# Scores in pairs, unbroken blocks on TensorE, and all weights' low halves by one VectorE operation, in a block-sparse attention with an FFN behind it

## The chip, the cores and the metric

The kernel runs on one core of one Trainium2 chip. The metric is the device time of one execution in microseconds (us). Three runs of the kernel before gave 951.11, 952.15 and 955.74 us; their median is 952.15. One further execution was profiled.

A core has five engines that run side by side and wait for each other by semaphores: PE (TensorE, matrix multiplication, whose loads of the stationary operand are listed as PEld), DVE (VectorE), ACT (ScalarE), POOL (GpSimd) and SP (SyncE, which here issues the DMA transfers). Each takes its instructions in a fixed order.

## The reference

```python
B, H, S, D = 4, 8, 768, 64          # batch, heads, sequence, head dimension
block = 32; n_blocks = 24; 3 sampled key blocks for each query block
scores = q @ k.transpose / sqrt(D)
mask  = neighbouring blocks (|i - j| <= 1), first and last block as query or key, sampled blocks
attn  = softmax(where(mask, scores, -1e9))
x     = (attn @ v) with the heads side by side          # 3072 tokens x 512
h     = x @ w_in                                        # 512 -> 2048
out   = maximum(0.01 * h, h) @ w_out                    # 2048 -> 512
```

All inputs and the output are float32 (the sampled blocks are integers).

## The kernel before

Every float32 operand of a matrix product is split into a high and a low half in float16, after a scaling by a power of two; a product is then three (FFN) or four (attention) matmuls in float16, added up in PSUM. A score is two matmuls for each head, with both halves stacked along the 128 rows.

**Attention.** The queries are cut into tiles of 64 (two blocks), 12 tiles (T = 0 to 11) for each batch, and the heads into four pairs hp. One *unit* is one tile and one pair of heads: 4 x 12 x 4 = 192 units. Tile 0 holds the first and the last block, which see all 768 keys: its units have two *parts* of 384 keys. All other units have one part, whose 384 keys (12 blocks of 32) are gathered into kg and vg beforehand. So there are 208 parts. Two neighbouring units (u.pi 0 and 1) are a *pair*; four tiles are an *item* of 256 tokens (12 items).

The way of a unit:

- `unit_scores` (L613 to L633): four matmuls a part into one of two PSUM buffers of the pool ps_s, each with 64 output columns of the array (128*64 in the profile), one for each head of the pair, once for qs and once for qxs.
- `unit_ttr` (L639, DVE): mask and scaling, the row's extreme mx; with it the PSUM buffer is free again. `unit_exp` (L650, ACT): the exponential and its sum. `pair_norm` (L658, L659, DVE): the reciprocals for both units of a pair.
- `unit_high` (L665, ACT) and `unit_split` (L670, DVE): the high and the low half of the probabilities, pp; then a transposing DMA from SP's queue (L673) into pt.
- `pair_av` (L691, PE): 24 matmuls for a pair (12 a unit), again 64 columns wide. `tile_evac` (L700 to L711) makes x from it.

**FFN.** It goes in chunks of two 128-wide slices of the hidden dimension, 8 chunks for each item: `ffn_h` (24 matmuls, L726), `ffn_act1`, `ffn_max`, `ffn_act2` (ACT L733, DVE L737 and L742, POOL L743) and `ffn_o` (12 matmuls, L753). Both use the full 128*128 array. 96 chunks are 2304 and 1152 matmuls.

**Weights.** w_in and w_out are loaded in eight parts (four quarters of each), decoded in place by ACT and DVE (L292 to L298), their scale found by matmuls of each block with itself (L172) and L175, and then split in `finish` (L340). ACT writes the high half (L353). For the low half there are two ways, chosen by a letter of `CFG["wsplit"]` for each part: "p" scales the raw values in place on ACT (L355) and subtracts on POOL (L356); "d" does both in one SCALAR_TENSOR_TENSOR on DVE (L358). Parts 0 to 5 come in two groups of 1024 columns each, parts 6 and 7 in four of 512; the last part always takes a third way (L348 to L351).

**Order of the work.** The main loop makes one step for each unit. In each step it emits pieces in the order of `CFG["ord"]`, "dtsixScmgovabphw": among them t (unit_ttr), s (split), S (the scores of the next unit), o (ffn_o), a (the attention-times-V of a pair at least three steps old), h (ffn_h) and w (some of the weights' work). Every emitted instruction has a priority that grows with the emission (`tc.cur_priority`). A planner then fixes each engine's order: it walks through the instructions by a model of their durations, and gives each engine the ready one of the smallest priority. So what is emitted as one block, 24 matmuls of h for instance, may be broken by other instructions that become ready in between.

The functions that the diff touches, and what calls them:

Of the kernel before, what the change touches and what calls it, by code (L numbers as in the profile page):

```python
# [13 lines left out]
F32 = mybir.dt.float32  # L14
# [5 lines left out]
P = 128  # L20
# [8 lines left out]
KEYS = SLOTS * BLOCK  # L29
# [20 lines left out]
    "rmin": 0.0,  # L50
    "side": 1.2,
    "side0": 1.6,
    "spread": 8,
    "v_at": 28,
    "wr": [(0, 1.0), (4, 3.0), (10, 4.0), (18, 4.5)],
    "wsplit": "ppppppdd",
    "xbufs": 3,
}

# [2 lines left out]
def tile_block_sparse_attention_ffn(  # L62
# [87 lines left out]
    def scales(ss, n, name, **how):  # L150
        now = tc.cur_priority
        tc.cur_priority = now - CFG["bs"]
        begin = len(nc.cur_bb.bb.instructions)
        pb = scale_sum(ss, n, name)
        loose.update(i.name for i in nc.cur_bb.bb.instructions[begin:])
        r = scale_of(pb, n, name, **how)
        tc.cur_priority = now + 8
        return r

    eye = cst.tile([P, P], BF16, name="eye")  # L160

# [448 lines left out]
    class Unit:  # L610
        pass

    def unit_scores(u):  # L613
        i, c0 = u.k // 2, u.k % 2 * Q2
        require_qk(u.b, u.j, i, u.hp)
        if u.T:
            require_kg(u.b, u.T)
        key = (u.b, u.j, i, u.hp)
        if key not in nscale:
            score_scale(*key)  # L620
        u.nsc = nscale[key]
        qs, qxs, _ = qstack[u.b, u.j, i]
        u.sp = []
        for part in range(u.parts):
            sp = ps_s.tile([P, 512], F32, tag="s", name=f"s_{u.nm}_{part}")[:, :KEYS]
            for n, st in enumerate((qs, qxs)):
                for hh in range(2):
                    h = 2 * u.hp + hh
                    keys = kgs[u.b, u.T][0][:, h, :] if u.T else kts[u.b][:, h, part * KEYS:(part + 1) * KEYS]
                    nc.tensor.matmul(  # L630
                        sp[hh * D:(hh + 1) * D, :], st[:, h, c0:c0 + Q2], keys,
                        start=(n == 0), stop=(n == 1))
            u.sp.append(sp)  # L633

    def unit_ttr(u):
        u.p = [pa.tile([P, KEYS], F32, tag="p", name=f"p_{u.nm}_{i}", bufs=CFG["p"]) for i in range(u.parts)]
# [42 lines left out]
    def pair_av(pr):  # L679

        if pr.hp == 0:
            avs[pr.item.n, pr.T] = bank(f"av_{pr.nm}", "av").rearrange("p (n l t) -> p n l t", n=NP, l=2)
        pr.av = avs[pr.item.n, pr.T]
        for u in pr.units:
            require_v(u.b, u.hp, u.T)
            n = NCH * u.parts
            for c in range(n):
                for l in range(2):
                    for hh in range(2):
                        vt = vgs[u.b, u.T][:, c, 2 * u.hp + hh, :] if u.T else v16s[u.b, u.hp][:, c, hh, :]  # L690
                        nc.tensor.matmul(  # L691
                            pr.av[hh * D:(hh + 1) * D, u.hp], vt[:, l * D:(l + 1) * D],
                            u.pt[c // NCH][:, :, c % NCH, hh * D:(hh + 1) * D],
                            start=(c == 0 and l == 0), stop=(c == n - 1 and l == 1))

    def tile_evac(pr):

# [20 lines left out]
    def ffn_h(c):  # L718
        it = c.item
        c.ph = bank(f"h_{it.nm}_{c.f}").rearrange("p (f t) -> p f t", f=2)  # L720
        for i in range(2):
            f = c.f + i
            b, o = f // PER, (f % PER) * P
            for d in range(NP):
                for m, (wl, xl) in enumerate(((1, 0), (1, 1), (0, 0))):
                    nc.tensor.matmul(  # L726
                        c.ph[:, i], W16[:, 2 * b, d, wl, o:o + P], it.x[:, xl, d, :],
                        start=(d == 0 and m == 0), stop=(d == NP - 1 and m == 2))

    def ffn_act1(c):  # L730
        scale = down[c.f // PER] if c.whole else (GDOWN, 0.01 * GDOWN)
# [12 lines left out]

    def ffn_o(c):
        it = c.item
        for t in range(N2 // P):
            if c.first:
                it.po[t] = ps_o.tile([P, DM], F32, tag="o", name=f"o_{it.nm}_{c.f}_{t}")
            for i in range(2):  # L750
                f = c.f + i
                for m, (gl, wl) in enumerate(((0, 1), (0, 0), (1, 1))):
                    nc.tensor.matmul(  # L753
                        it.po[t], c.g[:, gl, i, t * P:(t + 1) * P], W16[:, 2 * (f // PER) + 1, f % PER, wl, :],
                        start=(c.first and i == 0 and m == 0), stop=(c.last and i == 1 and m == 2))
            if c.last:
                outs.append((it, t, it.po[t], c.qs))

    betas = {}

# [53 lines left out]
    def require_qk(b, j, i, hp):  # L814
        until(("k", b, hp), lambda: (b, hp) in kready)
        until(("q", b, j, i), lambda: (b, j, i) in qstack)

    def require_kg(b, T):
        for hp in range(NP):
            until(("k", b, hp), lambda: (b, hp) in kready)  # L820
        until(("kg", b, T), lambda: (b, T) in kgs)
# [177 lines left out]
    for u in units:  # L999
        it, ui = u.item, u.k * NP + u.hp  # L1000
        b, nb = it.b, it.b + 1

        if step == 2:
            start_q(1)
        if step == 6 or step % 8 == 3 and step > 8:
            get_q((step + 5) // 8 + 1)
        if step % 8 == 6:
            start_q(step // 8 + 2)
        if nb < B:
            g = it.j * 16 + ui  # L1010
            t = g - (CFG["k_at"] if b else CFG["k_at0"])
            if t % 5 == 0 and 0 <= t // 5 < NP:
                get_k(nb, t // 5)
            if t % 5 == 3 and 0 <= t // 5 < NP:
                start_k(nb, t // 5)
            t = g - CFG["v_at"]
            if t in (0, 2, 4, 6):
                load_v(nb, t // 2)
            if t == 8:
                start(("v", nb), prep_v(nb))  # L1020

        if u.hp == (CFG["g_at"] if step >= 4 else NP - 1) and u.T + 1 < NT:
            start_gather(b, u.T + 1)
        tc.cur_priority = max(tc.cur_priority, 1000 + step * 200)
        if step in ready:
            add_ffn(ready.pop(step))
        refill()
        backlog = len(hq) + sum(len(t[1]) for t in tasks)
        credit += max(CFG["rmin"], min(CFG["rmax"], backlog / CFG["spread"]))
        n = int(credit)  # L1030
        credit -= n
        if step == 0:
            unit_scores(u)
        c = aq[0] if aq else None
        for w in CFG["ord"]:
            if w == "c" and c:
                ffn_act1(c)
            elif w == "m" and c:
                ffn_max(c)
            elif w == "g" and c:  # L1040
                ffn_act2(c)
                oq.append(aq.popleft())
            elif w == "S" and step + 1 < len(units):
                unit_scores(units[step + 1])
            elif w == "t":
                while live[0] + u.parts > CFG["p"]:
                    if not pend_high and not pend_split:
                        norm_step()
                    high_step()
                    split_step()  # L1050
                live[0] += u.parts
                unit_ttr(u)
            elif w == "x":
                unit_exp(u)
                if u.pi == 1:
                    pend_norm.append(u.pair)
            elif w == "d":
                norm_step()
            elif w == "i":
                high_step()  # L1060
            elif w == "s":
                split_step()
            elif w == "a":
                av_step()
                if vq and vfree[0] and (vq[0][0], "ready") in scr:
                    start_gather_v()
            elif w == "v":
                ev_step()
            elif w == "b":
                do_out()  # L1070
            elif w == "o":
                do_o(CFG["flag"] if hq or aq else 0)
            elif w == "p":
                side_step(CFG["side0"] if step < 16 else CFG["side"])
                gather_step(2)
            elif w == "w":
                wcredit += [r for a, r in CFG["wr"] if step >= a][-1]
                while wcredit >= 1.0:
                    c = next(weights, "end")
                    wcredit -= c if c != "end" else wcredit  # L1080
            elif w == "h":
                for i in range(n):
                    if i:
                        do_act()
                        do_o(CFG["flag"])
                    do_h()
        step += 1
        if ui == 15:
            ready[step + CFG["lead"] if it.n else step + CFG["lead0"]] = it
# [62 lines left out]
```

## Time and profile before

| | |
|---|---|
| median of three runs | 952.15 us |
| the profiled execution's own time | 950.05 us |
| its span, first to last instruction | 948.4 us |
| mean granted TensorE clock | 0.928 |
| PE busy | 780.1 us, 82% |
| DVE busy | 625.1 us, 66% |
| ACT busy | 492.7 us, 52% |
| POOL busy | 329.0 us, 35% |
| last decoding of weights (L298) ends | 204.9 us |
| last L639 of attention ends | 873.8 us |

A row of the groups reads: source line, engine, operation, out<-in by the program's names, shapes, xcount, then busy time in all and mean ns of one, then the engine's idle time just before them and what ended it. A row of the timeline reads: start and length in us, engine, line, operation, names, shape, xcount of the merged instructions, and in brackets the idle time before it with what released it. Ends of matmuls are modelled and overlap the next one's start, so starts are what to compare. A row of the waits reads: who waited, for whom, us in total, times, longest. In the slices, one digit is the busy share of a fortieth of the span (23.7 us) in tenths, and PEclk is the granted clock in tenths of full speed.

### The profile page before, as it was taken

Reading aid. Unit: us, or ns where it says so; the run is one execution under the profiler, and the core shown is the slowest. Engines: PE = TensorE matmul, PEld = TensorE weight load, DVE = VectorE, ACT = ScalarE, POOL = GpSimd, SP = SyncE. Lnnn points to the kernel's source line nnn. Section 1 sums busy time; section 2 is a strip of 40 time slices with the busy share of each in tenths; the row PEclk is TensorE's granted clock in tenths of the full one; section 3 lists DMA queues with packets and bytes.
Section 4 is the critical chain, followed back from the end, with each engine's and each line's share of the span. In section 5 each row is a group of like instructions: output and inputs, shape, how many; then the busy total and the mean of one; then the engine's idle time right before and its main releaser. Section 6 shows DMA issues by size and latency. Waiting matters only on the chain. (4 is left out here: it accounts for less than half of the span.)

```text
span 948.4 us, 21924 instructions
## 1 busy us (share of the span) xinstructions
PE 780.1 (82%) x7020; PEld 491.3 (52%) x7020; DVE 625.1 (66%) x1691; ACT 492.7 (52%) x1061; POOL 329.0 (35%) x469
## 2 busy tenths in 40 slices
PE   1335536889979988989989878997998989999998
PEld 0213324445646545655556545654555555656674
DVE  4889699998767866556666666566566766655221
ACT  4566656675545545546544645555445654545121
POOL 0134554542213434343414242442314342432221
PEclk9996657789998989999999989999999999999999
DMA  9995698777877766776884978866784765655200
GB/s 212 289 277 142 160 254 183 152 155 140 162 176 139 149 140 140 157 125 138 148 167 110 175 132 141 162 133 137 151 163 112 149 137 127 119 122 124 34 23 23
DMA packets 358129, 139.39 MB, mean 147 GB/s; under 512 B 323965, under 2 KB 336254, under 8 KB 358014
## 3 DMA queue, kind: packets, MB, share of 16 engines
q1 hardware_dynamic: 358014, 137.99, 69.7%
q8 instruction: 55, 0.90, 0.4%
q14 instruction: 60, 0.49, 0.2%
HBM read 65.57 MB, written 12.58 MB: 82 GB/s over the span
## 5 line engine op out<-in xcount | busy, mean ns | idle before, releaser
L726 PE MATMUL h<-x,W 128*128 128x256 f16 x2304 | 294.2, 284 | 0.4 <-DVE ht L737 0.4
L753 PE MATMUL o<-W,g 128*128 128x512 f16 x1152 | 281.1, 386 | 3.6 <-DVE ob L773 1.4
L726 PEld LDWEIGHTS <-W 128*128 128x128 f16 x2304 | 228.6, 103 | 55.0 <-issue 8.0
L670 DVE SCALAR_TENSOR_TENSOR pp<-p,r,pp 128x384 f16<-128x384 f32 x208 | 153.0, 746 | 131.4 <-ACT pp L665 130.5
L743 POOL TENSOR_TENSOR g<-ht,g 128x512 f16<-128x512 f32 x96 | 116.3, 1212 | 289.1 <-DVE g L742 199.4
L665 ACT ACTIVATE pp<-p,r 128x384 f16<-128x384 f32 x208 | 121.5, 608 | 142.3 <-DMA pt<-pp 105.7
L575 POOL COPY kg<-kt 128x256 f16 x264 | 127.6, 505 | 145.2 <-PE s L630 91.0
L753 PEld LDWEIGHTS <-g 128*128 128x128 f16 x1152 | 105.1, 99 | 134.9 <-issue 25.3
L650 ACT ACTIVATE p<-p,mx 128x384 f32<-128x384 f32 x208 | 126.5, 608 | 88.6 <-DVE mx L639 56.3
L691 PE MATMUL av<-pt,vg 128*64 128x128 f16 x2112 | 97.6, 233 | 33.1 <-DMA pt<-pp 26.5
L639 DVE CUSTOM_DVE_ANT_0 p<-s,em,nsc 128x384 f32<-128x384 f32 x176 | 106.3, 609 | 23.3 <-PE s L630 22.0
L691 PEld LDWEIGHTS <-vg 128*64 128x64 f16 x2112 | 78.6, 117 | 70.4 <-issue 58.5
L630 PE MATMUL s<-kg,qs_q 128*64 128x384 f16 x352 | 66.5, 367 | 26.8 <-DVE mx L639 25.1
L737 DVE SCALAR_TENSOR_TENSOR ht<-h,gd,ht 128x512 f32<-128x512 f32 x80 | 59.6, 745 | 41.5 <-ACT ht L733 41.1
L733 ACT ACTIVATE ht<-h,gs 128x512 f32<-128x512 f32 x80 | 54.2, 677 | 60.9 <-PE h L726 50.2
L711 POOL TENSOR_TENSOR x<-xf,x 128x256 f16<-128x256 f32 x48 | 35.7, 744 | 128.7 <-ACT x L709 128.4
L630 PEld LDWEIGHTS <-qs_q 128*64 128x64 f16 x416 | 28.8, 115 | 93.0 <-issue 63.1
L630 PE MATMUL s<-kg,qxs_q 128*64 128x384 f16 x352 | 65.0, 352 | 0.0
L742 DVE CAST g<-ht 128x512 f16<-128x512 f32 x96 | 41.5, 432 | 8.8 <-PE o L753 7.8
L506 ACT ACTIVATE qn_q<-rq 128x512 f16<-128x512 f32 x24 | 15.1, 628 | 55.4 <-DMA rq<-in_q_dram 55.2
L650 ACT ACTIVATION_READ_ACCUMULATOR p<-p,mx 128x1 f32 x208 | 39.0, 187 | 0.0
L658 DVE TENSOR_SCALAR sum<-sum 128x2 f32<-128x2 f32 x96 | 24.9, 259 | 19.0 <-ACT p L650 18.4
(128 smaller groups left out, 744.4 us busy)
## 6 DMA issues: line engine op xcount, KB each, us to landing
vg<-scr SPq DMA_DIRECT2D x280, 64.0 KB, 1.9
vg<-scr SPq DMA_DIRECT2D x44, 256.0 KB, 3.0
v<-in_v_dram SPq DMA_DIRECT2D x32, 192.0 KB, 3.4
scr<-v SPq DMA_DIRECT2D x16, 384.0 KB, 3.6
W<-in_moe_w_in_dram SPq DMA_DIRECT2D x5, 1024.0 KB, 6.7
rq<-in_q_dram SPq DMA_DIRECT2D x20, 256.0 KB, 3.7
out_dram<-ob SPq DMA_DIRECT2D x20, 256.0 KB, 2.4
rk<-in_k_dram SPq DMA_DIRECT2D x24, 192.0 KB, 3.4
```

What stands on the lines that cost most here:

```text
L575: nc.gpsimd.tensor_copy(out=kg[:, :, slot * BLOCK:(slot + 1) * BLOCK], in_=kt[:, :, bass.ds(off, BLOCK)])
L630: nc.tensor.matmul(sp[hh * D:(hh + 1) * D, :], st[:, h, c0:c0 + Q2], keys, start=(n == 0), stop=(n == 1))
L639: nc.vector.tensor_tensor_reduce(out=u.p[i], in0=u.sp[i], in1=kgs[u.b, u.T][1] if u.T else zero.to_broadcast([P, KEYS]), scale=u.nsc, scal ...
L650: nc.scalar.activation(u.p[i], u.p[i], AF.Exp, scale=-1.0, bias=u.mx[:, :1], accum_out=u.pair.sum[:, u.pi, i:i + 1])
L665: nc.scalar.activation(pp[:, 0, :], p, AF.Copy, scale=u.r)
L670: nc.vector.scalar_tensor_tensor(out=pp[:, 1, :], in0=p, scalar=u.r, in1=pp[:, 0, :], op0=ALU.mult, op1=ALU.subtract)
L691: nc.tensor.matmul(pr.av[hh * D:(hh + 1) * D, u.hp], vt[:, l * D:(l + 1) * D], u.pt[c // NCH][:, :, c % NCH, hh * D:(hh + 1) * D], start=( ...
L726: nc.tensor.matmul(c.ph[:, i], W16[:, 2 * b, d, wl, o:o + P], it.x[:, xl, d, :], start=(d == 0 and m == 0), stop=(d == NP - 1 and m == 2))
L733: nc.scalar.activation(c.t, c.ph, AF.Copy, scale=scale[1])
L737: nc.vector.scalar_tensor_tensor(out=c.t, in0=c.ph, scalar=scale[0], in1=c.t, op0=ALU.mult, op1=ALU.max)
L743: nc.gpsimd.tensor_tensor(out=c.g[:, 1], in0=c.t, in1=c.g[:, 0], op=ALU.subtract)
L753: nc.tensor.matmul(it.po[t], c.g[:, gl, i, t * P:(t + 1) * P], W16[:, 2 * (f // PER) + 1, f % PER, wl, :], start=(c.first and i == 0 and m ...
```

## The change

Three things are changed.

1. `unit_scores` becomes `scores(us)`, which takes a list of units. At a step with u.pi == 1 the scores of the next two units, which are the next pair, are emitted together, the second unit's matmuls first; at a step with u.pi == 0 nothing is emitted, since that unit's partner was done with it. Units of tile 0 (two parts each) still come one by one.
2. A new function `together` takes a list of emitters. All instructions after the first get a priority far ahead of everything else, and an order edge that places them behind the first. So the planner starts a block when its first instruction is its turn, and then places the others before anything else that is ready. It is used for the scores, for `pair_av` (where the second unit's matmuls now come first), for `ffn_h` and for `ffn_o`.
3. `wsplit` is "dddddddd": parts 0 to 5 take the way with one DVE operation too.

```diff
+    "spair": 1,
-    "wsplit": "ppppppdd",
+    "wsplit": "dddddddd",
...
+    def together(emits):
+        now = tc.cur_priority
+        begin = len(nc.cur_bb.bb.instructions)
+        for n, emit in enumerate(emits):
+            if n == 1:
+                tc.cur_priority = now - 100000
+            emit()
+        new = nc.cur_bb.bb.instructions[begin:]
+        for i in new[1:]:
+            tc.add_manual_dep(i, new[0].name, mybir.DependencyInfo(
+                mybir.DependencyClass.NoSync, mybir.DependencyReason.DATA), reason="together")
+        tc.cur_priority = now + len(new)
...
-    def unit_scores(u):
+    def scores(us):
+        emits = []
+        for u in us:
...
+            u.sp = [ps_s.tile([P, 512], F32, tag="s", name=f"s_{u.nm}_{part}")[:, :KEYS] for part in range(u.parts)]
+        for u in us[::-1]:
...
+                        emits.append(lambda o=sp[hh * D:(hh + 1) * D, :], a=st[:, h, c0:c0 + Q2], k=keys, n=n:
+                                     nc.tensor.matmul(o, a, k, start=(n == 0), stop=(n == 1)))
+        together(emits)
...
     def pair_av(pr):
...
+        for u in pr.units[::-1]:
...                       # the 24 matmuls as emitters, in the order c, l, hh as before
+        together(emits)
...
     def ffn_h(c):         # and ffn_o(c): the same matmuls in the same order as emitters
...
+        together(emits)
...
             elif w == "S" and step + 1 < len(units):
-                unit_scores(units[step + 1])
+                ahead = units[step + 1:step + 3]
+                if not CFG["spair"]:
+                    scores(ahead[:1])
+                elif u.pi == 1:
+                    if any(x.parts > 1 for x in ahead):
+                        for x in ahead[:1]:
+                            scores([x])
+                    else:
+                        scores(ahead)
+                elif u.parts > 1:
+                    scores(ahead[:1])
```

More of the change, by code (lines that the diff above doesn't have):

```diff
@@ L611, in tile_block_sparse_attention_ffn @@
         pass
-    def unit_scores(u):
[L614 to L633, printed above, removed]
+    def scores(us):
+        emits = []
+        for u in us:
+            i, c0 = u.k // 2, u.k % 2 * Q2
+            require_qk(u.b, u.j, i, u.hp)
+            if u.T:
+                require_kg(u.b, u.T)
+            key = (u.b, u.j, i, u.hp)
+            if key not in nscale:
+                score_scale(*key)
+            u.nsc = nscale[key]
+            u.sp = [ps_s.tile([P, 512], F32, tag="s", name=f"s_{u.nm}_{part}")[:, :KEYS] for part in range(u.parts)]
+        for u in us[::-1]:
+            i, c0 = u.k // 2, u.k % 2 * Q2
+            qs, qxs, _ = qstack[u.b, u.j, i]
+            for part, sp in enumerate(u.sp):
+                for n, st in enumerate((qs, qxs)):
+                    for hh in range(2):
+                        h = 2 * u.hp + hh
+                        keys = kgs[u.b, u.T][0][:, h, :] if u.T else kts[u.b][:, h, part * KEYS:(part + 1) * KEYS]
+                        emits.append(lambda o=sp[hh * D:(hh + 1) * D, :], a=st[:, h, c0:c0 + Q2], k=keys, n=n:
+                                     nc.tensor.matmul(o, a, k, start=(n == 0), stop=(n == 1)))
+        together(emits)
     def unit_ttr(u):
@@ L685, in pair_av @@
             require_v(u.b, u.hp, u.T)
+        emits = []
+        for u in pr.units[::-1]:
             n = NCH * u.parts
@@ L690, in pair_av @@
                         vt = vgs[u.b, u.T][:, c, 2 * u.hp + hh, :] if u.T else v16s[u.b, u.hp][:, c, hh, :]
[L691 to L694, printed above, removed]
+                        emits.append(lambda o=pr.av[hh * D:(hh + 1) * D, u.hp], a=vt[:, l * D:(l + 1) * D],
+                                     m=u.pt[c // NCH][:, :, c % NCH, hh * D:(hh + 1) * D], c=c, l=l, n=n:
+                                     nc.tensor.matmul(o, a, m, start=(c == 0 and l == 0), stop=(c == n - 1 and l == 1)))
+        together(emits)
     def tile_evac(pr):
@@ L720, in ffn_h @@
         c.ph = bank(f"h_{it.nm}_{c.f}").rearrange("p (f t) -> p f t", f=2)
+        emits = []
         for i in range(2):
@@ L725, in ffn_h @@
                 for m, (wl, xl) in enumerate(((1, 0), (1, 1), (0, 0))):
-                    nc.tensor.matmul(
-                        c.ph[:, i], W16[:, 2 * b, d, wl, o:o + P], it.x[:, xl, d, :],
-                        start=(d == 0 and m == 0), stop=(d == NP - 1 and m == 2))
+                    emits.append(lambda i=i, d=d, m=m, w=W16[:, 2 * b, d, wl, o:o + P], x=it.x[:, xl, d, :]:
+                                 nc.tensor.matmul(
+                                     c.ph[:, i], w, x, start=(d == 0 and m == 0), stop=(d == NP - 1 and m == 2)))
+        together(emits)
     def ffn_act1(c):
@@ L746, in ffn_o @@
         it = c.item
+        emits = []
         for t in range(N2 // P):
@@ L752, in ffn_o @@
                 for m, (gl, wl) in enumerate(((0, 1), (0, 0), (1, 1))):
-                    nc.tensor.matmul(
-                        it.po[t], c.g[:, gl, i, t * P:(t + 1) * P], W16[:, 2 * (f // PER) + 1, f % PER, wl, :],
-                        start=(c.first and i == 0 and m == 0), stop=(c.last and i == 1 and m == 2))
+                    emits.append(lambda o=it.po[t], i=i, m=m, a=c.g[:, gl, i, t * P:(t + 1) * P],
+                                 w=W16[:, 2 * (f // PER) + 1, f % PER, wl, :]:
+                                 nc.tensor.matmul(
+                                     o, a, w, start=(c.first and i == 0 and m == 0),
+                                     stop=(c.last and i == 1 and m == 2)))
             if c.last:
                 outs.append((it, t, it.po[t], c.qs))
+        together(emits)
     betas = {}
@@ L1032, in tile_block_sparse_attention_ffn @@
         if step == 0:
-            unit_scores(u)
+            scores([u])
         c = aq[0] if aq else None
```

## The prediction, made before the changed kernel was run

> **What bounds the kernel now.** I read the engine table and the slices first, then the windows, then the end of the chain.
>
> ```profile
> span 948.4 us, 21924 instructions
> PE 780.1 (82%) x7020; PEld 491.3 (52%) x7020; DVE 625.1 (66%) x1691; ACT 492.7 (52%) x1061; POOL 329.0 (35%) x469
> PE   1335536889979988989989878997998989999998
> DVE  4889699998767866556666666566566766655221
> PEclk9996657789998989999999989999999999999999
> ```
> ```profile
> 50.00:200.00 150.00, 85.54 (x822) 58.04 (x821) 135.22 (x302) 95.84 (x183) 73.03 (x83) 0.74 0.81 193
> 300.00:900.00 600.00, 552.01 (x5094) 341.41 (x5094) 372.21 (x1031) 309.06 (x704) 214.52 (x329) 0.97 0.69 136
> ```
> ```profile
> 900.13 2.70 PE o L753 x12
> 902.83 7.86 PE h L726 x72
> 918.49 2.62 PE h L726 x24
> 921.11 2.59 PE o L753 x12
> ```
>
> The columns of a window are its length, then the busy time of PE, weight loads, DVE, ACT and POOL, then the granted clock. There are two stages. From 50 to 200 us DVE is busy 135.22 of 150 (90%) with the weights' decoding and attention together, while PE does 85.54 at a clock of 0.74. From 300 to 900 us PE is busy 552.01 of 600 (92%) and DVE 372.21 (62%). The chain's last stretch is FFN alone on PE, unbroken: one h block of 24 matmuls takes 2.62 us and one o block of 12 takes 2.59 us. So the end is set by PE: the work it has, plus the idle time before 900 us. The first stage counts because a delay there moves all later PE work.
>
> **The change, part one: fewer switches of PE between two shapes.** Scores (s) and attention-times-V (av) use 64 columns of the array; h and o use 128. I call a run of s and av between h or o an island.
>
> ```profile
> 604.69 0.35 PE L630 MATMUL s<-kg,qs_q 128*64 128x384 f16 x2
> 604.88 0.33 PE L630 MATMUL s<-kg,qxs_q 128*64 128x384 f16 x2
> 605.14 2.76 PE L753 MATMUL o<-W,g 128*128 128x512 f16 x12
> 607.83 0.86 PE L691 MATMUL av<-pt,vg 128*64 128x128 f16 x24
> 608.62 2.79 PE L726 MATMUL h<-x,W 128*128 128x256 f16 x24
> 611.35 0.35 PE L630 MATMUL s<-kg,qs_q 128*64 128x384 f16 x2
> ```
> ```profile
> 634.50 0.33 PE L630 MATMUL s<-kg,qs_q 128*64 128x384 f16 x2
> 634.66 0.33 PE L630 MATMUL s<-kg,qxs_q 128*64 128x384 f16 x2
> 634.82 0.33 PE L630 MATMUL s<-kg,qs_q 128*64 128x384 f16 x2
> ```
>
> Starts are to be compared, since ends overlap. From 608.62 to 611.35 the h block before a score takes 2.73 us, 0.11 more than the 2.62 above. From 605.14 to 607.83 an o block before av takes 2.69, 0.10 more than 2.59. The lone score unit from 604.69 to 605.14 takes 0.45, where two steps inside a run of scores take 2 x 0.16 = 0.32: 0.13 more. One island therefore costs about 0.10 + 0.13 = 0.23 us. Breaking an h by an o has no such price (both have 128 columns), so unbroken h and o gain only where an island sat inside.
>
> How many go? Counted over the rows of PE from 200 to 900 us there are 209 islands; the first and the last are:
>
> ```profile
> 204.36 0.35 PE L630 MATMUL s<-kg,qs_q 128*64 128x384 f16 x2 [2.52 <-DVE mx L639]
> 899.27 0.86 PE L691 MATMUL av<-pt,vg 128*64 128x128 f16 x24
> ```
>
> 40 of the 208 score tiles precede the first. The 168 left are 24 of the first query tile of batches 1 to 3 (12 units of two parts, which the change doesn't pair) and 144 others, 72 pairs. With one island for a pair's scores and one for its av that is 144, plus 12 and 6 for the unpaired: 162. So 47 go, at 0.23 us: 10.8 us of PE. Ends of the range: none, if the planner still spreads them; and if scores and av always touched, one per pair, 72 fewer again, 27 us. I take 47, since the order list puts o between S and a. By PE's share in 300 to 900 (0.92) 9.9 us of it reaches the end; the rest falls into stretches where PE waits anyway. The rule in the Trainium skill, TensorEngine Tiling (Array Packing), section Key Properties, says that a change of tiling mode drains the engine while another tile of the same mode does not. The rows above agree, 0.10 us each way; by it a score beside an av would be free too, which is the 27 us end.
>
> **Part two: what the blocks wait for.** The two PSUM score buffers are freed by DVE's L639. Before, a unit's scores needed only the L639 of two units ago. Now the block's first matmul is the second unit's (the list is reversed), so the block needs the L639 of the unit just before the pair. Queued behind it on PE are the rest of the block, then o, av and h; DVE's L639 of the new pair waits for it, then ACT's exp. And a score that becomes ready during an h block now waits up to 2.7 us. For av the reversal puts the later transpose first, so a pair waits once where it could wait twice.
>
> ```profile
> PE s L630 <- DVE mx L639: 18.0, 18, 2.6
> PE av L691 <- DMA pt<-pp: 16.5, 17, 2.1
> ```
>
> These are PE's waits from 200 to 900 us: total, times, longest. Mean score wait 18.0 / 18 = 1.0 us. The nearest row for av is 16.5 us over 17 times; if half of those are a first half's wait, 8 go. For the scores the slack is one pair's period, 700 us / 78 pairs = 9.0 us, against the block (8 matmuls, 0.77 us by the 0.45 and 0.32 above) and two L639 with DVE's other work between. DVE is 62% busy, so I expect some more score waits, about as much as av loses: I take 0 net, with ends -8 and +19 (20 more waits, see the rivals).
>
> What a wait costs beside its own length can be seen twice:
>
> ```profile
> 627.23 0.53 PE L691 MATMUL av<-pt,vg 128*64 128x128 f16 x12 [1.94 <-DMA pt<-pp]
> 628.35 4.43 PE L753 MATMUL o<-W,g 128*128 128x512 f16 x12
> 769.68 0.35 PE L630 MATMUL s<-kg,qs_q 128*64 128x384 f16 x2 [0.77 <-DVE mx L639]
> 770.30 2.79 PE L726 MATMUL h<-x,W 128*128 128x256 f16 x24
> ```
>
> After a wait of 1.94 us the next o block took 4.43 instead of 2.76, so the clock had dropped and 1.67 us more were lost; after 0.77 us the h block ran at its usual 2.79. So a wait near 2 us can cost almost double. The Trainium skill, TensorE: Matmul & The Clock Gate, Part 1, has the clock fall only after an idle window of about 3.4 us. By that rule none of the waits of these two rows (longest 2.6 us) would cost more than itself, and the slower rival below would stay at its bare price; the trace differs (1.94 us did it), and decides.
>
> **Part three: the low halves.** Twelve groups of 1024 columns lose an ACT pass and a POOL subtraction and gain one DVE operation.
>
> ```profile
> L356 POOL TENSOR_TENSOR W<-W 128x1024 f16<-128x1024 f32 x12 | 28.8, 2413 | 10.5 <-ACT W L355 10.5
> L355 ACT ACTIVATE W<-W,wo_s 128x1024 f32<-128x1024 f32 x6 | 6.8, 1135 | 0.0
> L355 ACT ACTIVATE W<-W,wi_s 128x1024 f32<-128x1024 f32 x6 | 6.7, 1136 | 0.0
> L358 DVE SCALAR_TENSOR_TENSOR W<-W,wi_s 128x512 f16<-128x512 f32 x4 | 2.9, 786 | 0.2 <-ACT W L353 0.2
> L490 DVE SCALAR_TENSOR_TENSOR W<-W,k_s 128x768 f16<-128x768 f32 x4 | 4.0, 1018 | 0.9 <-ACT W L488 0.9
> ```
>
> Price of the new one: 1018 ns at 768 columns and 786 at 512 are 0.91 ns a column (232 / 256); 1018 + 256 x 0.91 is 1.25 us, and by proportion from 768 it is 1.36. I take 1.3: 12 x 1.3 = 15.6 us more on the engine that is 90% busy here. POOL loses 28.8 us and ACT 13.5. But those subtractions also hold DVE up:
>
> ```profile
> 81.98 5.62 POOL L356 TENSOR_TENSOR W<-W 128x1024 f16<-128x1024 f32 x2
> 82.60 3.02 DVE L296 SCALAR_TENSOR_TENSOR W<-W 128x1024 int32<-128x1024 int32 x1
> 61.04 1.21 DVE L296 SCALAR_TENSOR_TENSOR W<-W 128x1024 int32<-128x1024 int32 x1
> 56.28 1.54 DVE L643 TENSOR_TENSOR mx<-mx 128x1 f32<-128x1 f32 x1
> 60.37 0.15 DVE L643 TENSOR_TENSOR mx<-mx 128x1 f32<-128x1 f32 x1
> 176.32 1.48 DVE L658 TENSOR_SCALAR sum<-sum 128x2 f32<-128x2 f32 x1
> ```
>
> The same L296 takes 3.02 us beside the subtraction and 1.21 without POOL; a one-column L643 takes 1.54 instead of 0.15. Sixteen DVE operations lie so over an L356, the first at 56.28 and the last at 176.32; over each one's usual time they lose 18.3 us together. So DVE's balance is +15.6 - 18.3 = -2.7 us, of which 90% counts: -2.4. Behind each new operation on DVE stand the decoding of the next group and the attention's split, and the FFN on that quarter waits for it; before, the same waited for two ACT passes and 2.4 us of POOL. Ends: +15.6, if none of the 18.3 comes back, and -13, if ACT's 13.5 us also shorten the chain through exp and its copies. ACT is busy 95.84 of 150, so I count that at nothing; if ACT were the one waited for, that is the gain left out. No DMA is moved, and SP's queue keeps its issues.
>
> **Sum.** Against the profiled execution's own 950.05 us: -9.9 + 0 - 2.4 = 937.7. The median of the runs, 952.15, is 2.1 above that execution, so I forecast 940 us.
>
> **Rivals.** (a) Slower: the scores come too late. Place: PE before a pair's block. Mean price 1.0 us a wait; the gain is 12.3 us, so it decides from 13 more waits among 78 pairs on; with 32 more, which is under half of the pairs, 940 + 32 = 972, and with 20 it is 960. For it: 18 waits on L639 already with a unit of lead more, and the drop of the clock after 1.94 us. Against it: the 9.0 us period, and DVE's 62%.
> (b) Slower: the lock time isn't won back, since DVE, ACT and PE wait for each other in a ring there; then 952.15 - 9.9 + 15.6 = 958. For it: DVE at 90%. Against: twelve operations of 1.3 us replace sixteen held up by more.
> (c) No change: the planner, who decides the order by its own costs, leaves about 209 islands or moves the saving into waits; 952.15 - 2.4 = 950. For it: 82% busy PE in the whole span, and 34.5 us of the two waits above to absorb a gain of 10.
>
> **How the numbers follow.** No change can be told from the measurement within 0.5%, 947.4 to 956.9 us. The forecast's case has 0.57, with a range of its own from 926 (both lower ends in part: -8 for av and -6 for ACT) to 947. (a) has 0.17, of which 0.02 (few waits more) ends within 0.5%; (b) 0.08, all slower; (c) 0.18, of which 0.03 is just faster than 947.4 and 0.15 within. So faster 0.57 + 0.03 = 0.60, same 0.15 + 0.02 = 0.17, slower 0.15 + 0.08 = 0.23. The range 926 to 962 leaves out (a) beyond 22 more waits, some 0.10, and gains of more than 24 us, some 0.07.
>
> **What would show it.** Right: about 160 islands from 200 to 900 us, most scores in runs of eight; PE's busy time some 11 us lower; no L356 and L355, twelve L358 more near 1.3 us, no L296 or L643 of over 2 us beside POOL; the stage before 200 us no longer than now. Wrong: score waits on L639 well above 18 us, granted clock below 0.97 in the middle, later weights, or the islands still near 200.

## The result, and the profile after

The changed kernel is 0.6% slower: 957.2 us in the median of 17 runs, against 950.88 us for 17 runs of the kernel before; ratio 1.0062, 95% interval 1.0045 to 1.0079. I had forecast 940 us. The time lies in the range, on the wrong side.

The profiled execution took 955.13 us. Its engine table and PE's slices:

```profile
span 953.2 us, 21854 instructions
PE 760.9 (80%) x7020; PEld 492.8 (52%) x7020; DVE 629.1 (66%) x1703; ACT 477.7 (50%) x1049; POOL 304.9 (32%) x457
PE   1333436777997987998888876998988989999998
```

The two windows that stood in the prediction, of the changed kernel (length, busy PE, weight loads, DVE, ACT, POOL, then granted clock, share of the DMA engines, GB/s):

```profile
50.00:200.00 150.00, 80.11 (x780) 54.54 (x779) 126.44 (x301) 84.29 (x174) 46.08 (x66) 0.69 0.83 190
300.00:900.00 600.00, 534.19 (x5048) 345.14 (x5043) 381.67 (x1042) 308.25 (x708) 215.33 (x337) 0.97 0.69 137
```

PE's busy time fell by 19.2 us (780.1 to 760.9), and yet the span grew by 4.8. PE has less to do and waits longer. A piece of its order, from the timeline of the changed kernel:

```profile
607.18 0.86 PE L713 MATMUL av<-pt,vg 128*64 128x128 f16 x24
607.97 2.76 PE L778 MATMUL o<-W,g 128*128 128x512 f16 x12
610.57 2.78 PE L748 MATMUL h<-x,W 128*128 128x256 f16 x24
613.29 0.35 PE L650 MATMUL s<-kg,qs_q 128*64 128x384 f16 x2
613.47 0.33 PE L650 MATMUL s<-kg,qxs_q 128*64 128x384 f16 x2
613.64 0.33 PE L650 MATMUL s<-kg,qs_q 128*64 128x384 f16 x2
613.80 0.33 PE L650 MATMUL s<-kg,qxs_q 128*64 128x384 f16 x2
614.06 2.76 PE L778 MATMUL o<-W,g 128*128 128x512 f16 x12
```

That is what the change was to make: av, o and h whole, eight score matmuls in a run (0.77 us from 613.29 to 614.06). From 200 to 900 us 124 islands are left of 209, the first at 201.97 us, the last at 889.35. The low halves take the time that I had worked out (row below), and no L356 is left to hold DVE up. DVE is busy 126.44 of 150 us from 50 to 200, where it had 135.22, but over the whole execution it has 4.0 us more (629.1 against 625.1), so most of that difference is work that now comes later:

```profile
L373 DVE SCALAR_TENSOR_TENSOR W<-W,wo_s x6: 1258/1274/1415, 80.5 to 171.0; 128x1024 f16<-128x1024 f32 x6
```

(Shortest, median and longest in ns.) The three parts of the change do what they say. What was missing is a gain at the end.

### The profile page after: what moved, and what is told of

The parts are those of the page before. It is cut to its first block, busy times and chain, and to the rows that moved or that the text cites. A ratio compares the mean times of both kernels' runs of the same rounds, so it can differ in the third digit from the quotient of the medians.

```text
span 953.2 us, 21854 instructions
## 1 busy us (share of the span) xinstructions
PE 760.9 (80%) x7020; PEld 492.8 (52%) x7020; DVE 629.1 (66%) x1703; ACT 477.7 (50%) x1049; POOL 304.9 (32%) x457
## 5 line engine op out<-in xcount | busy, mean ns | idle before, releaser
L748 PE MATMUL h<-x,W 128*128 128x256 f16 x2304 | 277.1, 278 | 2.6 <-DVE k_tot L137 1.4
L688 DVE SCALAR_TENSOR_TENSOR pp<-p,r,pp 128x384 f16<-128x384 f32 x208 | 138.4, 681 | 129.6 <-ACT pp L683 127.9
L683 ACT ACTIVATE pp<-p,r 128x384 f16<-128x384 f32 x208 | 121.4, 608 | 130.6 <-DMA pt<-pp 104.0
L778 PEld LDWEIGHTS <-g 128*128 128x128 f16 x1152 | 107.9, 100 | 147.2 <-issue 21.2
L713 PE MATMUL av<-pt,vg 128*64 128x128 f16 x2112 | 87.2, 234 | 40.8 <-DMA pt<-pp 30.2
L713 PEld LDWEIGHTS <-vg 128*64 128x64 f16 x2112 | 74.8, 119 | 72.0 <-issue 51.1
L657 DVE CUSTOM_DVE_ANT_0 p<-s,em,nsc 128x384 f32<-128x384 f32 x176 | 103.3, 610 | 10.9 <-PE s L650 9.9
L676 DVE TENSOR_SCALAR sum<-sum 128x2 f32<-128x2 f32 x96 | 27.0, 281 | 31.7 <-ACT p L668 30.9
```

Of the source, the lines that this page charges most:

```text
L657: nc.vector.tensor_tensor_reduce(out=u.p[i], in0=u.sp[i], in1=kgs[u.b, u.T][1] if u.T else zero.to_broadcast([P, KEYS]), scale=u.nsc, scal ...
L683: nc.scalar.activation(pp[:, 0, :], p, AF.Copy, scale=u.r)
L688: nc.vector.scalar_tensor_tensor(out=pp[:, 1, :], in0=p, scalar=u.r, in1=pp[:, 0, :], op0=ALU.mult, op1=ALU.subtract)
L713: nc.tensor.matmul(o, a, m, start=(c == 0 and l == 0), stop=(c == n - 1 and l == 1)))
L748: nc.tensor.matmul(c.ph[:, i], w, x, start=(d == 0 and m == 0), stop=(d == NP - 1 and m == 2)))
L778: nc.tensor.matmul(o, a, w, start=(c.first and i == 0 and m == 0), stop=(c.last and i == 1 and m == 2)))
```

## The experiments

All ratios are to the kernel before, run beside each kernel on the same chip, with a 95% interval in brackets. Line numbers of a row are those of its own kernel. My first two theories were: (A) the twelve DVE operations delay the stage up to 230 us; (B) the blocks and pairs do, because PE then waits in front of a block with the scores behind it.

**Which part of the change costs?**

```diff
 e1_low_halves_only: the kernel before with
+    "wsplit": "dddddddd",
 e2_pairs_and_blocks_only: the changed kernel with
+    "wsplit": "ppppppdd",
 e3_no_pairs: the changed kernel with
+    "spair": 0,
 e4_no_blocks: the changed kernel, in together()
-            if n == 1:
-                tc.cur_priority = now - 100000
...
-        for i in new[1:]:
-            tc.add_manual_dep(i, new[0].name, ...)
 e5_blocks_only: the changed kernel with "spair": 0 and "wsplit": "ppppppdd"
```

> The kernel before with all low halves on DVE, scores and blocks as before. The changed kernel is 6 us slower, its weights are ready 10 us later (last decoding-stage operation on W at 226.8 us against 217.2) although DVE was less busy from 50 to 200 us (126.4 against 135.2). Theory A: the twelve DVE operations cause the delay, since they stand in DVE's order ahead of decoding and attention: then this kernel is 6 to 12 us slower than before (957 to 963) and its last operation on W is near 227. Theory B: the delay comes from PE's order (blocks whose first matmul waits for the later of two units, with the scores queued behind it); then this kernel is within 4 us of before, or up to 4 faster (947 to 952), last operation on W at 213 to 218.

> The changed kernel with the low halves of parts 0 to 5 on ACT and POOL again; pairs and unbroken blocks stay. Theory A: without the DVE operations the early delay is gone and the gain of fewer islands shows: 940 to 946. Theory B: the delay stays, last operation on W at 225 or later, 955 to 962; PE's waits for the transposes (av on pt) from 50 to 200 us stay near 30 us against 14.7 before.

> The changed kernel with the scores emitted one unit a step again; blocks and low halves as changed. If the pairing of the scores (which need the L657 of the unit just before) is what costs, 943 to 950, and the score waits on L657 fall from 46 us to 36 or less. If the unbroken av blocks are what costs, still 955 to 960. Islands from 200 to 900 us between 124 and 209, I expect 180.

> The changed kernel with the function that holds blocks together reduced to plain emission, so that the planner may break av, scores, h and o; pairs, the reversed order within a pair and low halves as changed. If unbroken blocks cost (an av block stands ahead of the scores until its first transpose lands), 943 to 950, and PE's av waits on pt fall from 39 us to about 31. If pairing costs, 955 to 962, score waits on L657 near 46 us.

> The kernel before with the unbroken blocks alone: scores one unit a step, low halves as before. So far: low halves alone 1.0046 of before, pairs and blocks 1.0016, blocks with low halves 1.0015, pairs with low halves but no blocks 1.0140, all three 1.0062. If the three parts add up, blocks alone stand at 1.0015 - 0.0046 = 0.997: 945 to 949. If every change of the order costs the stage up to 230 us some microseconds whatever it is, 950 to 953.

Measured: low halves alone 1.0046 (1.0025 to 1.0066), 953.93 us; pairs and blocks alone 1.0016 (0.9991 to 1.0041); without pairs 1.0015 (0.9991 to 1.0038); without blocks 1.0140 (1.0098 to 1.0183); blocks alone 1.0008 (0.9986 to 1.0030). So the low halves carry 0.46% of the 0.62%, and pairs with blocks neither gain nor clearly lose (0.16%, within its interval); the two add up. Neither theory's times were met: the low halves alone lie between theory A's 957 to 963 us and theory B's 947 to 952, pairs and blocks alone (952.09 us) between A's 940 to 946 and B's 955 to 962. For A speaks that the low halves alone make the weights late: their last copy (L351, L366 in the changed kernel) starts at 227.8 us, against 219.1 in the kernel before and 228.7 in the changed one. But late weights aren't the loss by themselves, since without pairs it starts at 228.3 us too, at a ratio of 1.0015. That blocks alone leave the time as it was went against the sum that I had expected of them (945 to 949). Pairs without blocks, with the low halves on DVE, are the worst of these five.

**Does the late part gain by itself?** Pairs and blocks from step 43 on, with everything before it in the order of the kernel before:

```diff
+    "late": 43,
...
+            if n == 1 and step >= CFG["late"]:
...
+                if not CFG["spair"] or step < CFG["late"]:
```

> Pairs and blocks only from step 43 on (after some 230 us), everything earlier and the low halves as before; each engine's order up to there is that of the kernel before. Theory C (all the loss arises up to 230 us; later the fewer islands pay, but PE's waits take most of it back): the late part gains 3 to 6 us, 944 to 948. Theory D (pairs and blocks cost as much as they gain in the late part too): 949 to 953. My prediction's sum, if PE's work were the bound from 230 us on, would give 938 to 941.

Measured 1.0008 (0.9988 to 1.0029): no gain, as theory D had it. The rows from 230 to 900 us, before and then this kernel:

```profile
230.00:900.00 670.00, 613.46 (x5653) 380.64 (x5651) 419.87 (x1166) 344.15 (x782) 230.50 (x351) 0.96 0.70 139
```
```profile
230.00:900.00 670.00, 595.48 (x5658) 382.60 (x5656) 426.46 (x1167) 343.05 (x783) 227.94 (x351) 0.96 0.69 139
```

PE needs 18.0 us less for as many matmuls (5658 against 5653), and nothing of it reaches the end. PE's work isn't the bound of this stretch.

**Is it PE's wait for the transposes?** In the low-halves kernel PE waits 37.8 us for them up to 230 us, against 14.7 before, so I put av one step later up to step 42, with the low halves and, as a control, without:

```diff
-                pend_av.append((step + CFG["av_lag"], pu.pair))
+                pend_av.append((step + CFG["av_lag"] + (step < 43), pu.pair))
```

> The low halves on DVE alone, and up to step 42 each attention-times-V block emitted one step later, so that its transposes have longer to land. In the low-halves kernel PE waits 37.8 us for them up to 230 us (14.7 before), and the scores, ACT's copy and DVE's xf stand behind. If this wait is what makes the low halves slower, it falls below 20 us here, and the time goes from 953.9 back to 947 to 951. If it is the decoding chain on DVE, the time stays at 952 to 957.

> The kernel before with the same one step more for attention-times-V up to step 42: the control for the run with the low halves. If a later av is good in itself, 945 to 949, waits on pt up to 230 us below 14.7; if the order before is simply a lucky one and any shuffle costs, 952 to 957.

Measured: 1.0010 (0.9986 to 1.0034) with the low halves, 1.0031 (1.0009 to 1.0052) on the kernel before. The time of the first came back as expected, but the wait didn't go: 32.5 us (row below), where I had set below 20. In the control it even grew, from 14.7 to 26.9 us.

```profile
PE av L691 <- DMA pt<-pp: 32.5, 14, 8.0
```

So this wait as the cause isn't shown. What the pair of runs suggests is the size of such effects: the same edit of the order goes with 0.36% less on one kernel (not clear of noise: its two intervals overlap from 1.0025 to 1.0034) and puts 0.31% on another.

**Who is late, then?** Two views that I hadn't asked before the prediction: SyncE's own waits, and the rows of the DMA issues. First the kernel before, 230 to 900 us, SyncE's queue and then one row of ACT:

```profile
SPq L673 <- PE s L630: 20.0, 20, 2.0
SPq L673 <- PE av L691: 16.6, 16, 1.5
SPq L673 <- DVE g L742: 7.0, 9, 1.2
SPq L673 <- DVE pp L670: 6.4, 5, 1.5
```
```profile
ACT pp L665 <- DMA pt<-pp: 103.0, 49, 6.4
```

L673 is the transpose of pp into pt. What it needs is the finished pp, by DVE's L670, and a free pt, which PE's av gives back. For L670 SyncE waits only 5 times, 6.4 us: nearly always pp is ready before SyncE comes to it. ACT in turn waits 103.0 us for one of the four pp buffers, which the transposes free. All rows of SyncE's waits in this view add up to 129.0 of the 670 us, most of them of about a microsecond, so the queue isn't occupied without a gap. What SyncE does with one transpose and one gather of v (shortest, median, longest in ns), and how it looks in order, with one row of DVE and one of ACT from the same time:

```profile
L673 SPq DMA_TRANSPOSE pt<-pp x208: 1209/1238/2823, 58.0 to 881.5; - x104
```
```profile
L605 SPq FUSED_REGOPS  x264: 37/37/52, 69.6 to 878.2; - x132
L605 SPq MOVE vg<-scr x264: 29/29/38, 69.7 to 878.3; - x132
L605 SPq DMA_DIRECT2D vg<-scr x264: 315/316/952, 69.8 to 878.4; - x132
```
```profile
L603 SPq TENSOR_LOAD <-offs x264: 262/272/646, 26.2 to 877.7; - x132
L603 SPq FUSED_REGOPS  x264: 152/152/187, 26.7 to 878.0; - x132
L603 SPq SEQ_ASSERT  x264: 18/18/28, 27.0 to 878.2; - x132
```
```profile
329.38 2.55 SPq L673 DMA_TRANSPOSE pt<-pp  x2
332.91 0.35 SPq L595 DMA_DIRECT2D vg<-scr  x1
333.51 6.29 SPq L605 DMA_DIRECT2D vg<-scr  x6
339.91 1.27 SPq L673 DMA_TRANSPOSE pt<-pp  x1
```
```profile
332.81 0.61 DVE L670 SCALAR_TENSOR_TENSOR pp<-p,r,pp 128x384 f16<-128x384 f32 x1
342.76 0.61 ACT L665 ACTIVATE pp<-p,r 128x384 f16<-128x384 f32 x1 [4.14 <-DMA pt<-pp]
```

208 transposes of 1.238 us are 257 us; 264 gathers of 0.82 us (six rows, their medians added) are 218 us. Together 475 us of the 823 from the first transpose to the last, before any other transfer is issued, and a run of six gathers (6.29 us from 333.51) keeps a pp waiting that DVE had finished at 333.42: no transpose starts before 339.91, and ACT, which needs a free pp, stands idle for 4.14 us until 342.76. SyncE isn't counted as busy anywhere on the page. Hence theory E: its queue sets the pace.

```diff
 e10_before_gathers_on_act: the kernel before with
-            off = nc.sync.value_load(offs[:1, i:i + 1], ...)
+            off = nc.scalar.value_load(offs[:1, i:i + 1], ...)
...
-            nc.sync.dma_start(out=vg[ps, c, :], in_=scr[b][bass.ds(off, BLOCK), :])
+            nc.scalar.dma_start(out=vg[ps, c, :], in_=scr[b][bass.ds(off, BLOCK), :])
 e11_before_gathers_on_pool: the same with nc.gpsimd
 e12_late_gathers_on_act: the late pairs and blocks with the edit of e10
 e13_after_gathers_on_act: the changed kernel with the edit of e10
```

> The kernel before with the 264 gathering transfers of v (register load and issue, some 0.83 us of SP each by the rows of L603 and L605) moved from SP's queue to ACT's. In 300 to 900 us SP's own rows add up to 501 of 600 us, as much as PE's share, and a transpose waits there behind a run of six gathers (6.3 us). Theory E: SP's queue sets the pace of attention from 230 us on, and so a lighter PE gains nothing: then this kernel gains at least 5 us (below 945), and PE's waits on pt fall below 20 us from 31. Theory F: the pace is set by latencies round the ring and not by SP's queue: 948 to 955, or slower, since 264 x 0.83 = 219 us go to an ACT that is busy 52%.

> The same with the gathers on POOL's queue (35% busy). Theory E: below 945 too. Theory F: 948 to 960; POOL then also shares its time with the key gathers and the lows of g.

> Pairs and blocks from step 43 on, with the gathers of v on ACT's queue. Theory E: with SP relieved the fewer islands pay: 8 us or more faster than the kernel with the gathers on ACT alone. Theory F: within 4 us of it.

> The changed kernel with the gathers of v on ACT's queue. Theory E: its 6 us behind the kernel before vanish or turn, 940 to 948. Theory F: it stays 4 to 8 us behind the kernel before with the gathers on ACT.

Measured: the kernel before with the gathers on ACT 0.9785 (0.9751 to 0.9819), 928.1 us, and PE's waits on pt fell from 31.2 to 12.4 us, as theory E had it; late pairs and blocks 0.9713 (0.9684 to 0.9741), 921.27 us; the changed kernel 0.9481 (0.9452 to 0.9510), **898.82 us**, faster than both kernels of this case and by far more than theory E's 940 to 948. With the gathers on POOL 1.0624 (1.0586 to 1.0661), where theory E had a gain: ACT's wait for a free pp falls there too, from 105.7 to 6.3 us, but the gathers take POOL 134.2 us and POOL stands idle for 167.6 us just before them (row below). That POOL is what makes it slower is likely and not shown by a run. The late part is worth 0.7% here, 6.8 us, a little less than the 8 I had set for theory E.

```profile
L605 POOL DMA_DIRECT2D vg<-scr x264 | 134.2, 509 | 167.6 <-issue 119.2
```

The waits turn round as theory E needs it. SyncE's own and ACT's for pp, 230 to 900 us, in the changed kernel with the gathers on ACT:

```profile
SPq L691 <- DVE pp L688: 86.0, 30, 8.7
```
```profile
ACT pp L683 <- DMA pt<-pp: 4.2, 5, 1.8
```

Now SyncE waits for the data (86.0 us; 4.1 in the changed kernel with SyncE loaded), and ACT no longer for the transposes (4.2 us; there it was 104.0). All of SyncE's waits add up to 397.3 of the 670 us, where they were 117.2.

**Which part of the change pays then?** The edit of e10 on each part alone:

> The low halves on DVE alone, scores and blocks as before, gathers of v on ACT's queue. With the gathers there, the kernel before stands at 0.9785 of before and the changed one at 0.9481, so the change is worth 3.1%. If the low halves carry half of that (ACT, which now issues the gathers, loses 13.5 us of scaling passes, and POOL 28.8), this kernel stands near 0.963 (914). If they are neutral or cost as before, 0.978 to 0.983 (929 to 933).

> Pairs and blocks over the whole run, low halves on ACT and POOL as before, gathers of v on ACT's queue. From step 43 on alone they stand at 0.9713. If the low halves carry half of the 3.1%, this kernel is at 0.963 to 0.971 (914 to 922); if pairs and blocks carry all, near 0.948 (900).

| | gathers on SyncE | gathers on ACT |
|---|---|---|
| as before | 1 | 0.9785 (0.9751 to 0.9819) |
| low halves on DVE | 1.0046 (1.0025 to 1.0066) | 0.9653 (0.9618 to 0.9687) |
| pairs and blocks | 1.0016 (0.9991 to 1.0041) | 0.9609 (0.9575 to 0.9643) |
| both | 1.0062 (1.0045 to 1.0079) | 0.9481 (0.9452 to 0.9510) |

In the right column the low halves are worth 0.9653 / 0.9785 = 0.987, pairs and blocks 0.982, both 0.969 (from the ends of the two intervals, 0.963 to 0.975). The same edits that cost 0.6% on the left bring 3.1% on the right.

**Is it SyncE and not ACT?** Moving work changes two queues, so one kernel loads SyncE alone: each gather as two transfers of half the columns, the same bytes. And one asks whether the fixed rows of vg should go over as well.

```diff
 e16_gathers_in_halves: the kernel before with
+            for x in (slice(0, H * D), slice(H * D, 2 * H * D)):
+                nc.sync.dma_start(out=vg[ps, c, x], in_=scr[b][bass.ds(off, BLOCK), x])
 e17_after_all_of_v_on_act: e13 with the other transfers into vg on nc.scalar too
```

> The kernel before with each of the 264 gathers of v issued as two transfers of half the columns, the same bytes in all, so that SP's queue has 264 more issues of 0.32 us (L605's median): 84 us more. Theory E (SP's queue sets the pace): slower by half of that or more, 990 us and up. If ACT was what helped in the runs with the gathers on ACT, and SP's queue has room, 948 to 960.

> The changed kernel with all transfers into vg on ACT's queue, the fixed rows too (L610, L615: some 50 issues of about half a microsecond). With the gathers on ACT it stands at 0.9481. If SP's queue is still near the pace, 3 to 10 us more: 889 to 896. If PE is the bound now, 896 to 901.

Measured 1.1339 (1.1313 to 1.1364), 1078.12 us: 127 us more for 264 x (316 + 46 + 29) ns = 103 us of SyncE (medians of that kernel's three rows a transfer). So added work on this queue goes into the kernel's time in full; why it is 24 us more than that stays open. It doesn't hold the other way: the kernel before lost some 218 us of issues on this queue and gained 21 us (949.14 to 928.1), so something else sets the pace soon after. ACT has no work added here, and it waits 161.4 us for a free pp from 230 to 900 us (103.0 before). The DMA engines are less loaded than before, 60.6% against 69.7%, so it isn't their bandwidth:

```profile
q1 hardware_dynamic: 370686, 138.01, 60.6%
```

Nor is it the way of the data. One could think that the gathers' bytes hold up those of the transposes, and that a second queue helps by letting them pass. The transposes' median time from issue to landing says otherwise; here are the kernel before, the one with the gathers on ACT, and the one with halved gathers:

```profile
pt<-pp SPq DMA_TRANSPOSE x208, 3.1
pt<-pp SPq DMA_TRANSPOSE x208, 3.6
pt<-pp SPq DMA_TRANSPOSE x208, 2.8
```

Once issued they land later in the faster kernel and sooner in the slower one, so what counts is when they are issued.

The last kernel came to 0.9774 (0.9751 to 0.9796), 928.61 us, 30 us behind e13 and outside both ranges. The fixed rows wait for their buffer, and on ACT everything stands behind that wait: ACT's two largest waits of this kind are 63.0 and 31.8 us (rows below), where e13 has 23.6 and 53.2. That is 18.0 us more together; the rest of the 30 isn't explained.

```profile
ACT ht L755 <- DMA vg<-scr: 63.0, 10, 9.1
ACT p L668 <- DMA vg<-scr: 31.8, 7, 7.4
```

The Trainium skill, DMA: Bandwidth & Descriptors, section Issuing engines are not separate DMA queues, says that starting DMAs from several engines saves only the sequencer's time, which it calls usually small beside the transfer. The trace differs on the size here: one transpose takes 1.238 us of the sequencer and 3.1 us to land, and moving the gathers' issues was worth 2.15% to the kernel before.

## Why the prediction was wrong, point by point

- **What bounds the kernel.** The step that failed first. I read PE's 92% from 300 to 900 us as the bound. The late kernel has 18.0 us less of PE's work there and no gain. What held the time was SyncE's queue, which the engine table doesn't list; the prediction names it once, to say that it keeps its issues, and puts no price on it. With the gathers off it the kernel before took 0.9785 of its time, with more issues on it 1.1339. The sign was in the groups of the kernel before: ACT's largest wait, 105.7 us before L665, ended by the DMA pt<-pp. The prediction doesn't weigh it.

```profile
L665 ACT ACTIVATE pp<-p,r 128x384 f16<-128x384 f32 x208 | 121.5, 608 | 142.3 <-DMA pt<-pp 105.7
```

- **Fewer switches, 9.9 us.** The mechanism was right and even undersized: 85 islands fewer instead of 47, and 19.2 us of PE's busy time instead of 10.8. The price of 0.23 us an island held: 85 of them are 19.6 us, against the 19.2 measured. The factor 0.92, by which it was to reach the end, was wrong: with SyncE loaded it is about 0. With the gathers on ACT pairs and blocks are worth 1.8% of 928.1 us, 16.7 us, for 22.2 us less of PE's busy time (761.5 to 739.3). From step 43 on alone they bring 6.8 us for 12.6 (761.5 to 748.9), about half, so 0.92 isn't borne out there either.
- **What the blocks wait for, 0.** PE's score waits from 230 to 900 us rose from 14.9 to 23.9 us and its av waits fell from 16.5 to 8.8: about the exchange I had taken. New and unforeseen are av's waits on xf (none in the kernel before) and o's on g (0.2):

```profile
PE s L650 <- DVE mx L657: 23.9, 19, 5.0
PE av L713 <- DVE xf L723: 8.5, 7, 2.4
PE av L713 <- DMA pt<-pp: 8.8, 9, 2.6
PE o L778 <- DVE g L764: 8.2, 7, 1.8
```

- **Low halves, -2.4 us.** The price (1.27 us against 1.3) was right, and nearly all of the time that DVE lost beside POOL came back: with the low halves alone DVE's busy time went from 625.1 to 623.8 us over the whole execution, so 15.6 us were added and 16.9 won, of the 18.3 that I had taken. The sign of the effect was wrong: +0.46%. The balance on DVE isn't what decides: the weights are ready later (last subtraction of a low half at 226.8 us in the changed kernel against 217.2), with PE waiting more for transposes. That it pays 1.3% as soon as SyncE has room shows that the DVE operations themselves aren't the loss; that is 12.5 us, far beyond the forecast 2.4, and where they come from isn't worked out. Why it is a loss and not nothing with SyncE loaded stays open; the two kernels with a later av suggest that a mere shift in the order moves the time by some 0.3% there.
- **Rivals.** (b) has the nearest time, 958 us, by luck: its sum lets 9.9 us of the islands reach the end, where nothing did, and puts 15.6 us on DVE, which won 16.9 back. (c), that waits take the saving, is nearest in what happened, but the two waits that I named for it grew by only 1.3 us together (23.9 + 8.8 against 14.9 + 16.5). (a) puts the loss on the scores; their waits grew by 9 us only.

## What to carry to other kernels

Before a saving on the busiest engine is counted, look at the queue that issues the DMAs: add up its rows, and see whether it waits for its data or its data for it. Here it waited 6.4 us of 670 for its main input while ACT, which needs the buffers back, waited 103.0, and that one comparison would have called the forecast in question. A change that gains nothing behind one bound can be a good one behind another; try it again once the first is moved.

## What the runs showed of the hardware that I had not expected

- A transposing DMA costs 1.24 us of the issuing queue and a gather with an address from a register 0.82 us, so that 472 transfers (208 and 264) take half of a 950 us kernel on one queue.
- Added issues went into the time in full: 103 us of them cost 127 us, though SyncE still waited 83.0 of the 670 us from 230 to 900 there. A queue can set the pace without being occupied all the time.
- A switch between 128 and 64 columns costs PE about 0.10 us each way. With a lone score unit's slower start that is 0.23 us an island; the late pairs and blocks have 79 islands fewer from 200 to 900 us (130 of 209), 18.2 us by this price, and PE's busy time fell by 18.0.
